# Gated mix of windowed attention and token MLP on one core: a new written-out order of tasks and PSUM banks

## Chip, cores and metric

The kernel runs on one core of a Trainium2 chip, in bf16 with float32 sums in PSUM. The metric is the device time of one execution in microseconds (us). The core's engines are TensorE (PE in the profile; its weight loads are PEld), VectorE (DVE), ScalarE (ACT), GpSimd (POOL) and SyncE (SP), which here issues all DMAs.

## The reference

Two branches read the same x of 2048 tokens by 512 channels and are mixed by a gate per token. Branch A is attention with 32 heads of 16 channels, in which a token sees itself and the 255 tokens before it. Branch B normalises each token, then multiplies along the token axis: 2048 to 1376, gelu, 1376 to 2048.

```python
x = A_x
g = sigmoid((x * gate_w).sum(-1, keepdims=True))
# A
qkv = x @ wqkv                       # 2048 x 1536, 32 heads of 16
scores = q @ k.T * 16 ** -0.5        # per head
scores = where((i - j >= 0) & (i - j < 256), scores, -1e9)
a = (softmax(scores) @ v) @ wo
# B
h = layernorm(x)                     # over the 512 channels
u = gelu(einsum("bsd,sf->bdf", h, w1) + b1)
b = transpose(einsum("bdf,fs->bds", u, w2) + b2)
out = g * a + (1 - g) * b
```

## The kernel before

**Tiles.** Tokens are worked in 16 tiles of 128 and four blocks of 512. x is loaded as it is (`xo`, four tiles to a load) and transposed (`XT`: block 0 by TensorE, tasks `xta` and `xtc`, blocks 1 to 3 by DMA transposes, tasks `xt1` to `xt3`). `wqk0` to `wqk3` and `wv` load the projection weights, `w1_gi` the first MLP weights (group g of columns, block i of rows), `w2_g` the second ones into the same memory once the `u` chains of that group are done, `wo` the output weights.

**Tasks.** The program is a list of named tasks, each on one engine:

- `q k v`: projection chains, four matmuls into one PSUM bank, in pieces of two (`q1_2.0` and `q1_2.2` are quarter 1 of the channels for block 2; block 0's pieces are single matmuls, `.0` to `.4`). `qc`, `kc` and `vc` copy a chain's bank out; `qc` (DVE) spreads q over heads in `QZ`.
- `s{j}.v0` to `v3`, `s{j}.C`: scores of attention step j, whose 128 queries begin at 128 j + 64, with full key tiles (visits) and with the corners of the window; each fills two pairs of PSUM banks. `e` (ACT) takes the exponential of a pair, `m` (DVE or POOL) masks it, `pv{j}.0` to `.3` multiply with v. `n1`, `n2`, `nz`, `n3`, `n4` (DVE) normalise and write the result back into `xo`.
- `vs` and `vz` are small DMAs that place copies of v for the corners. They wait for value copies, on SP's queue.
- `bs`, `ba` (DVE) and `pow` (POOL) make the layernorm's mean and deviation, `h` (DVE) the normalised tile. `gate0` (TensorE) and `gl` (DVE) make the gate's sums, `gatee` its exponential; `biast` and `biasc` turn the biases into columns, and `gate0` waits for `biasc`.
- `u0` to `u10`: the first MLP product, 16 matmuls each in pieces of two, needing all 16 `h` and a whole group of w1. `ub` adds the bias. `gelu` is one task on ACT for all of them.
- `y0` to `y14`, `y15l`, `y15r`: the second MLP product (11 matmuls) and the attention's output product (4 matmuls, which wait for `n4`) in one bank; `f` applies gate and bias, `o` stores.

**Order.** It isn't left to a scheduler. `PLAN` (line 189) lists for each engine every task in order; digits behind a colon are the PSUM banks or buffers that it takes. `arrange` (line 85) walks these lists with planned durations and interleaves the engines' lists into one order of emission; the order within an engine is the list's. Where two engines use one PSUM bank after each other, the later one waits.

**Pieces in tiles.** A chain's piece that stands behind a score or pv task named in `THEN` is issued as matmuls of 32 weight columns, four times as many (`tiled[0]` in `chain`, lines 645 to 676), which avoids a change of array mode after pv. The matmuls of all chains carry line 670, of scores 942 (998 for the last step), of corners 1042, of pv 1087.

**Instruction blocks.** In `arrange`, `count` adds up TensorE's instructions, and a block of 256 that is planned to arrive late delays the planned start:

```python
while (block + 1) * BLOCK <= count + ins:
    block += 1
    at = start + t.cost * (block * BLOCK - count) / ins
    wait = max(0.0, come.get(block, 0.0) - at)
```

Of the kernel before, what the change touches and what calls it, by code (L numbers as in the profile page):

```python
# [9 lines left out]
ACT = mybir.ActivationFunctionType  # L10
# [68 lines left out]
SWITCH = 0.095  # L79

BLOCK, AHEAD, FETCH, BUSY = 256, 80, 3.6, 3.0
LATENCY = {"PE": 0.22, "ACT": 0.15, "DVE": 0.12, "POOL": 0.15, "SP": 2.0}


def arrange(tasks):
# [18 lines left out]
    mode, then = "d", "d"  # L104
    count, come, loads = AHEAD, {}, 0.0
    order = []
    while len(order) < len(tasks):
# [19 lines left out]
        t.cost = t.engines[e]  # L127
        ins = t.ins
        if e == "PE":
            new = then if t.flex else t.mode  # L130
            if new != mode:
                t.cost += SWITCH
            if t.flex and new == "p":
                t.tiled = True
                ins *= 4
            if t.mode != "d":
                then = "p" if t.name in THEN else "d"
            mode = new
        if e == "SP" and t.lat is not None and t.engines[e] > 1.0:
            loads = max(loads, start + t.cost + t.lat)  # L140
        if ins:
            block = count // BLOCK
            while (block + 1) * BLOCK <= count + ins:
                block += 1
                at = start + t.cost * (block * BLOCK - count) / ins
                wait = max(0.0, come.get(block, 0.0) - at)
                t.cost += wait
                come[block + 1] = at + wait + FETCH + (BUSY if at + wait < loads else 0.0)
            count += ins
# [41 lines left out]
        warm:3 xta0.0.0:7 xta0.0.1:6 warmb xta0.1.1:4 xta0.1.0:5 q1_0.0:2 k3_0.0:3 k1_0.0:6 q3_0.0:1 k0_0.0:7  # L191
        q3_0.1 q0_0.0:0 k3_0.1 q1_0.1 q1_0.2 k1_0.1 k3_0.2 k0_0.1 q0_0.1 q2_0.0:5 q1_0.3 q0_0.2 q1_0.4 q0_0.3
        k3_0.3 q3_0.2 q0_0.4 k3_0.4 q3_0.3 k2_0.0:4 q2_0.1 k0_0.2 k1_0.2 k1_0.3 k0_0.3 k1_0.4 q2_0.2 q3_0.4 q2_0.3
        k0_0.4 k2_0.1 k2_0.2 k2_0.3 k2_0.4 q2_0.4 s0.v0:62 q3_1.0:0 q3_1.2 k3_1.0:1 k3_1.2 q0_1.0:7 s0.C:42 v1.0:6
        q0_1.2 s-1.C:02 v1.2 v2.0:5 v2.2 s1.v3:02 biast:4 v0.0:7 v0.2 v3.0:5 v3.2 q1_1.0:4 s1.v0:62 v5.0:1 q1_1.2
        gate0:5 v5.2 v14.0:0 s0.v1:62 v13.0:5 k2_1.0:1 v14.2 pv-1.0:6 v10.0:4 k2_1.2 v13.2 s1.v2:26 k2_2.0:0 v10.2
        v15.0:1 v12.0:5 v12.2 v15.2 k2_2.2 pv0.0:2 pv0.1 s1.v1:64 pv0.2 v4.0:1 v4.2 k3_2.0:0 k3_2.2 s2.v1:26 v7.0:5
        v7.2 k0_2.0:4 s1.C:60 k0_2.2 v6.0:3 v6.2 s2.v3:06 k0_1.0:2 k0_1.2 k1_1.0:5 k1_1.2 pv1.0:6 pv1.1 pv1.2
        s2.v0:02 v11.0:4 v11.2 v8.0:5 v8.2 pv1.3 pv1.4 s2.v2:20 q2_1.0:5 v9.0:4 q2_1.2 s2.C:26 v9.2 k1_2.0:1 k1_2.2
        u3.0:0 u3.2 s3.v1:64 u3.4 u3.6 u3.8 s3.C:26 u3.10 u3.12 u3.14 u2.0:1 s3.v2:24 pv2.0:6 pv2.1 u7.0:0 pv2.2  # L200
        pv2.3 u7.2 u2.2 s3.v0:42 u2.4 u7.4 u7.6 s3.v3:46 u7.8 u7.10 u7.12 s4.v0:62 u2.6 u2.8 u2.10 u2.12 u2.14
        s4.v1:24 pv3.0:6 pv3.1 pv3.2 pv3.3 u7.14 u10.0:1 u10.2 s5.v2:42 u10.4 u10.6 u10.8 s4.v3:62 u10.10 q0_2.0:0
        q0_2.2 s4.v2:64 u10.12 u10.14 q3_2.0:2 u0.0:3 q3_2.2 s4.C:06 u0.2 u0.4 u0.6 s6.v0:40 u0.8 u0.10 u0.12
        u6.0:2 u0.14 s5.v0:06 pv4.0:4 pv4.1 pv4.2 pv4.3 u6.2 u6.4 q2_2.0:3 s5.v1:06 u6.6 q2_2.2 u6.8 s5.C:64 u6.10
        u6.12 u5.0:3 s6.C:60 u6.14 u5.2 u5.4 s6.v2:46 u5.6 k3_3.0:2 k3_3.2 q1_2.0:1 q1_2.2 u5.8 s5.v3:46 u5.10
        u1.0:2 u1.2 s6.v1:06 u1.4 pv5.0:4 u5.12 pv5.1 pv5.2 pv5.3 s6.v3:06 u1.6 u5.14 u1.8 s7.v0:64 u1.10 pv6.0:0
        pv6.1 pv6.2 u1.12 pv6.3 s7.v1:64 u1.14 u4.0:3 u4.2 s7.v3:06 u4.4 k1_3.0:2 k1_3.2 s7.C:04 u4.6 u4.8 q0_3.0:2
        s7.v2:60 q0_3.2 u4.10 u4.12 u4.14 s8.v3:46 u9.0:2 u9.2 u9.4 s8.C:04 u8.0:3 u8.2 u8.4 u8.6 s8.v1:46 u8.8
        u9.6 u9.8 s8.v0:04 u8.10 u9.10 u9.12 u8.12 u8.14 s8.v2:06 pv7.0:4 u9.14 pv7.1 pv7.2 pv7.3 s10.v0:02
        k0_3.0:7 k0_3.2 q1_3.0:4 q1_3.2 q3_3.0:6 k2_3.0:5 k2_3.2 q3_3.2 pv8.0:0 pv8.1 pv8.2 pv8.3 y4.0:3 q2_3.0:6  # L210
        q2_3.2 y0.0:7 y0.2 y0.4 y8.0:2 y0.6 y4.2 y0.8 s9.v1:40 y4.4 y8.2 y0.10 y8.4 y0.11 y0.13 s9.v3:40 y4.6 y4.8
        y4.10 y4.11 s9.v2:60 y4.13 y8.6 y8.8 s9.C:04 y7.0:3 y8.10 y7.2 y8.11 s9.v0:60 y7.4 y8.13 y7.6 s10.C:46 y7.8
        y2.0:2 y2.2 s10.v3:06 y2.4 y7.10 y2.6 y7.11 s11.v3:46 y2.8 y7.13 pv9.0:0 pv9.1 pv9.2 pv9.3 s10.v2:64 y2.10
        y2.11 y9.0:3 y9.2 s10.v1:04 y2.13 y9.4 y9.6 s11.C:60 y9.8 y1.0:2 y1.2 s11.v2:40 y1.4 y1.6 y9.10 y1.8
# [12 lines left out]
        e-1.C.0:b vc1 vc2 e1.v3.1:2 e1.v3.0:3 vc3 e1.v0.0:6 e1.v0.1:9 vc5 gatee0 e0.v1.0:d e0.v1.1:c vc14 kc2_1
        vc13 e1.v2.1:b e1.v2.0:7 vc12 vc15 kc2_2 e1.v1.0:5 e1.v1.1:a vc4 e2.v1.1:4 e2.v1.0:8 e1.C.1:d e1.C.0:c vc7
        vc6 e2.v3.1:1 e2.v3.0:0 kc1_1 e2.v0.1:a e2.v0.0:9 vc8 vc11 e2.v2.0:b e2.v2.1:5 e2.C.1:e vc9 e2.C.0:f
        e3.v1.0:c e3.v1.1:d e3.C.0:7 e3.C.1:6 ub3 e3.v2.0:a e3.v2.1:4 e3.v0.0:b e3.v0.1:5 e3.v3.1:f e3.v3.0:e  # L230
        e4.v0.1:1 e4.v0.0:0 e4.v1.0:b e4.v1.1:4 ub7 e5.v2.1:f e5.v2.0:e e4.v3.0:a e4.v3.1:d e4.v2.0:5 ub10
        e4.v2.1:c e4.C.0:2 e4.C.1:3 e6.v0.1:9 e6.v0.0:8 gatee1 e5.v0.1:0 e5.v0.0:1 e5.v1.1:c e5.v1.0:d e5.C.0:4
        e5.C.1:5 e6.C.0:7 e6.C.1:6 e6.v2.1:a e6.v2.0:b kc3_3 e5.v3.1:g e5.v3.0:h e6.v1.0:2 e6.v1.1:3 gatee2
        e6.v3.1:g e6.v3.0:h e7.v0.0:f e7.v0.1:e ub5 e7.v1.0:g e7.v1.1:d e7.v3.0:h e7.v3.1:c e7.C.0:9 e7.C.1:8
        e7.v2.0:a e7.v2.1:b e8.v3.0:6 e8.v3.1:7 e8.C.1:3 e8.C.0:4 e8.v1.0:2 e8.v1.1:5 e8.v0.0:1 e8.v0.1:0 gatee3
        e8.v2.0:f e8.v2.1:e e10.v0.0:g e10.v0.1:h gelu e9.v1.1:b e9.v1.0:8 e9.v3.1:9 e9.v3.0:2 e9.v2.1:4 e9.v2.0:3
        e9.C.0:5 e9.C.1:i e9.v0.0:a e9.v0.1:j e10.C.1:6 e10.C.0:f e10.v3.1:0 e10.v3.0:c e11.v3.0:1 e11.v3.1:d
        e10.v2.1:7 e10.v2.0:e e10.v1.0:5 e10.v1.1:4 e11.C.1:3 e11.C.0:j e11.v2.1:b e11.v2.0:a e11.v1.0:i e11.v1.1:2
# [1136 lines left out]
```

## Time and profile before

| quantity | value |
|---|---|
| median of three runs | 200.57 us (199.84 to 200.81) |
| profiled execution | 199.82 us |
| its span, first to last instruction | 198.1 us |
| instructions | 9100 |
| TensorE busy, granted clock | 193.0 us (97%), 1.0 |
| ACT busy | 169.0 us (85%) |
| DVE busy | 156.5 us (79%) |
| POOL busy | 80.0 us (40%) |
| moved by DMA | 22.02 MB, mean 111 GB/s |

The profile is of one execution. Busy time is the union of an engine's instructions; matmuls overlap, so the distance from one start to the next tells more of TensorE than its busy share. A timeline line gives the start, the time covered, the engine, the line of the kernel and the operation with its shapes and count. DMA issues on SP are marked SPq; their time is that of the issue, and the landing is listed apart.

### The profile page before, as it was taken

To read this page: it belongs to the slowest core of one execution; us is meant where nothing else is said; L and a number is where in the kernel's file an instruction comes from. 1 tells how busy PE (TensorE), PEld (TensorE's weight loads), DVE (VectorE), ACT (ScalarE), POOL (GpSimd) and SP (SyncE) were. 2 spreads that over 40 slices of the span, in tenths; PEclk is the share of its full clock that TensorE was granted. 3 is DMA by queue.
4 is the path that set the end of the run, shared out by engine and by line. 5 is a ranking of instruction groups with operands and counts; after the bars stand their busy time and mean duration, and the time that the engine had idled before them with its cause. 6 is when DMAs were issued, how large, how long until landed. Compare 5 with 4: busy or idle time off the path is not lost. (4 is left out here: it accounts for less than half of the span.)

```text
span 198.1 us, 9100 instructions
## 1 busy us (share of the span) xinstructions
PE 193.0 (97%) x4058; PEld 93.3 (47%) x4058; DVE 156.5 (79%) x318; ACT 169.0 (85%) x198; POOL 80.0 (40%) x118
## 2 busy tenths in 40 slices
PE   7999999999999999999999999999999999999993
PEld 3643444353635445446543554344445354554572
DVE  1799888879998988986589799636867868869683
ACT  2369999999988996998999899899899989898632
POOL 6394897525344440214223200045069335452310
PEclk9999999999999999999999999999999999999999
DMA  5999798970060000001399770000211220200002
GB/s 156 294 284 232 131 319 278 346 187 0 8 174 18 18 0 3 3 5 32 98 364 367 280 210 3 26 26 30 68 37 58 60 68 22 62 30 30 30 3 83
DMA packets 23189, 22.02 MB, mean 111 GB/s; under 512 B 7566, under 2 KB 21262, under 8 KB 23150
## 3 DMA queue, kind: packets, MB, share of 16 engines
q1 hardware_dynamic: 23150, 21.44, 36.9%
q8 instruction: 32, 0.52, 1.1%
q14 instruction: 7, 0.06, 0.1%
HBM read 15.61 MB, written 2.10 MB: 89 GB/s over the span
## 5 line engine op out<-in xcount | busy, mean ns | idle before, releaser
L894 ACT ACTIVATE et<-ps 128x1024 bf16<-128x1024 f32 (+1 forms) x94 | 89.3, 1015 | 6.1 <-PE ps L942 2.4
L536 POOL TENSOR_SCALAR_AFFINE_SELECT et<-et 128x512 bf16<-128x512 bf16 (+2 forms) x63 | 46.7, 751 | 56.0 <-ACT et L894 40.9
L894 ACT ACTIVATE XT<-ps 128x1024 bf16<-128x1024 f32 (+1 forms) x60 | 58.1, 1011 | 7.3 <-PE ps L942 4.3
L670 PEld LDWEIGHTS <-wb 128*32 128x32 bf16 (+4 forms) x645 | 32.0, 97 | 34.5 <-issue 6.5
L670 PE MATMUL pb<-ug,wb 128*32 128x512 bf16 (+4 forms) x385 | 45.5, 366 | 0.0
L670 PE MATMUL pb<-h,wb 128*128 128x512 bf16 (+2 forms) x260 | 44.5, 381 | 0.0
L536 POOL TENSOR_SCALAR_AFFINE_SELECT XT<-XT 128x512 bf16<-128x512 bf16 (+1 forms) x28 | 20.0, 720 | 46.3 <-ACT XT L894 27.4
L670 PE MATMUL pb<-XT,wqkv 128*128 128x512 bf16 (+2 forms) x190 | 32.4, 372 | 0.4 <-DMA wqkv<-in_A_wqkv_dram 0.3
L1178 DVE STREAM_TRANSPOSE et<-ps 128x1024 f32<-128x1024 f32 (+1 forms) x17 | 20.1, 1183 | 11.9 <-PE ps L1087 11.1
L1087 PEld LDWEIGHTS <-VA 128*32 128x32 bf16 (+1 forms) x1056 | 20.1, 97 | 6.6 <-issue 1.5
L942 PE MATMUL ps<-QZ,KT 32*128 32x256 bf16 (+1 forms) x496 | 23.1, 265 | 0.0
L754 DVE TENSOR_TENSOR QZ<-pb,par 128x1024 bf16<-128x1024 f32 x16 | 19.5, 1221 | 3.2 <-PE pb L670 3.2
L670 PEld LDWEIGHTS <-wqkv 128*128 128x128 bf16 (+1 forms) x190 | 12.7, 98 | 14.6 <-DMA wqkv<-in_A_wqkv_dram 0.5
L670 PE MATMUL pb<-wo,xo 128*32 128x512 bf16 (+2 forms) x152 | 18.1, 375 | 0.0
L1087 PE MATMUL ps<-et,VA 128*32 128x128 bf16 (+2 forms) x624 | 17.9, 218 | 0.0
L942 PEld LDWEIGHTS <-KT 32*128 32x128 bf16 x496 | 7.4, 92 | 20.6 <-ACT et L894 10.7
L670 PE MATMUL pb<-wqkv,XT 128*128 128x512 bf16 (+1 forms) x70 | 16.5, 381 | 0.0
L974 DVE TENSOR_TENSOR et<-et,mask 128x512 bf16<-128x512 bf16 x26 | 13.3, 510 | 2.5 <-ACT et L894 2.4
L441 DVE TENSOR_SCALAR ot<-pb,c,c 128x512 bf16<-128x512 f32 (+1 forms) x11 | 8.6, 785 | 7.4 <-PE pb L670 7.3
L1087 PE MATMUL ps<-XT,VA 128*32 128x128 bf16 (+2 forms) x432 | 13.9, 215 | 0.0
L1087 PEld LDWEIGHTS <-VZ 128*32 128x32 bf16 x832 | 13.2, 98 | 0.7
L770 DVE BATCH_NORM_STATS2 stats<-xo 128x6 f32<-128x512 bf16 x16 | 10.7, 682 | 3.1 <-DMA xo<-in_A_x_dram 3.1
(76 smaller groups left out, 199.4 us busy)
## 6 DMA issues: line engine op xcount, KB each, us to landing
wb<-in_B_w_dram SPq DMA_DIRECT2D x8, 512.0 KB, 8.2
wb<-in_B_w_dram SPq DMA_DIRECT2D x2, 2048.0 KB, 9.2
VZ<-VA SPq DMA_DIRECT2D x26, 70.0 KB, 3.0
xo<-in_A_x_dram SPq DMA_DIRECT2D x3, 512.0 KB, 5.5
out_dram<-ot SPq DMA_DIRECT2D x12, 128.0 KB, 2.4
wb<-in_B_w_dram SPq DMA_DIRECT2D x4, 352.0 KB, 5.8
wqkv<-in_A_wqkv_dram SPq DMA_DIRECT2D x4, 256.0 KB, 5.0
wb<-in_B_w_dram SPq DMA_DIRECT2D x1, 1024.0 KB, 5.3
```

Of the source, the lines that this page charges most:

```text
L441: return nc.vector.tensor_scalar(out=out_, in0=in_, scalar1=scale, scalar2=bias, op0=ALU.mult, op1=ALU.add)
L536: return nc.gpsimd.affine_select(out=out_, in_=in_, pattern=[[0, n] for n in pattern] + [[step, HB]], compare_op=op, fill=0.0, base=base_, ...
L670: made.append(nc.tensor.matmul(buf(b)[c:z_, c0:c0 + w_], lhsT=lhsT[:, c:z_], rhs=rhs, start=(j == 0), stop=(j == n - 1), skip_group_check= ...
L754: lambda k=k, b=b: nc.vector.tensor_tensor(out=QZ[:, k, :, (i % NQ) * SB:(i % NQ + 1) * SB], in0=buf(b)[:, None, :].to_broadcast([P, 2, SB ...
L770: f"bs{t_}", {"DVE": 0.67}, lambda b=b, t_=t_: nc.vector.bn_stats(buf(b)[:], xo[:, t_, :]),
L894: lambda e=e, b=b, shape=shape: nc.scalar.activation(out=shape(buf(e)), in_=shape(buf(b)), func=ACT.Exp, scale=SCALE),
L942: made.append(nc.tensor.matmul(to[:, :, done:done + m], lhsT=keys(j if x == "A" else j - 1, k)[rows], rhs=q[rows], start=True, stop=True, ...
L974: made.append(nc.vector.tensor_tensor(out=v, in0=v, in1=m.to_broadcast(list(v.shape)), op=ALU.mult))
L1087: return lambda: nc.tensor.matmul(to(), lhsT=v() if callable(v) else v, rhs=buf(e)[rows, col:col + n], start=first, stop=last, tile_positi ...
L1178: lambda: nc.vector.transpose(out=view(buf(tr).bitcast(FP32)), in_=view(buf(o))), [last], takes=[tr], uses=[o],
```

## The change

All five lists of `PLAN`, the bank and buffer digits in them, and `THEN` are replaced. So are the constants with which `arrange` plans: the cost of a change of array mode becomes a table by pair, task costs are corrected by `cost_of`, and the arrival of an instruction block is planned from the row that asks for it (77 rows ahead of the block) and needed 194 rows inside it, with a longer fetch while a large load runs. Planned durations of some loads, of `vs`/`vz`, of `gelu` and of the w2 loads change. No task is added or removed, and the code that emits instructions is the same.

```diff
-SWITCH = 0.095
-BLOCK, AHEAD, FETCH, BUSY = 256, 80, 3.6, 3.0
-LATENCY = {"PE": 0.22, "ACT": 0.15, "DVE": 0.12, "POOL": 0.15, "SP": 2.0}
+TURN = {
+    "d": dict(d=0, s=0.100, p=0.100, c=0.098, h=0.100),
+    "s": dict(d=0.116, s=0, p=0.115, c=0.105, h=0.114),
...
+}
+BLOCK, AHEAD, INSIDE, FETCH, BUSY = 256, 77, 194, 4.0, 2.4
+LATENCY = {"PE": 0.21, "ACT": 0.15, "DVE": 0.11, "POOL": 0.12, "SP": 2.3}
+def cost_of(t, e):
+    c, n = t.engines[e], t.name
+    if e == "PE":
+        return c - 0.02 if t.mode == "s" else c * 0.738 if t.mode == "c" else c
+    if e == "DVE":
+        return max(0.1, c - 0.06)
...
-            block = count // BLOCK
-            while (block + 1) * BLOCK <= count + ins:
...
+            for k in range(1, int(x1 / BLOCK) + 2):
+                at = BLOCK * k - AHEAD
+                if x0 <= at < x1:
+                    asked[k] = start + t.cost * (at - x0) / (x1 - x0)
...
     SP="""
-        x0.0 x0.2 wqk0 wqk1 wqk2 wqk3 x1.4 xt1 wv x2.8 bias xt3 x3.12 xt2 vs0 w1_02 w1_03 vs1 w1_22 vs2 gw w1_12
-        w1_23 w1_01 w1_00 w1_10 w1_11 vz2:0 w1_13 vz3:1 vz4:2 vz5:0 w1_20 w1_21 vz6:1 vz8:0 w2_0 vz7:2 w2_1 w2_2
+        x0.0 x0.2 wqk0 wqk1 x1.4 wqk2 wqk3 x2.8 wv xt1 bias xt3 x3.12 vs0 xt2 vs1 w1_21 w1_20 w1_03 w1_01 gw
+        vz2:1 vz4:0 vs2 w1_02 w1_12 w1_00 w1_22 w1_11 w1_10 vz3:2 vs13 w1_13 w1_23 vz7:1 vz5:2 vz6:0 w2_0
...
     PE="""
-        k0_0.4 k2_0.1 k2_0.2 k2_0.3 k2_0.4 q2_0.4 s0.v0:62 q3_1.0:0 q3_1.2 k3_1.0:1 k3_1.2 q0_1.0:7 s0.C:42 v1.0:6
+        q0_0.4 k3_0.2 k3_0.3 k3_0.4 q2_0.3 q2_0.4 q3_0.2 q3_0.3 q3_0.4 s0.v0:06 v2.0:2 v1.0:5 v2.2 v0.0:4
+        v1.2 s0.C:06 v5.0:3 v5.2 v0.2 k2_1.0:2 s-1.C:06 q3_1.0:5 q3_1.2 k2_1.2 s1.v3:06 v14.0:3 v4.0:4 v14.2
+        v4.2 biast:5 v3.0:2 s1.v0:06 v3.2 q1_1.0:4 q1_1.2 v12.0:7 gate0:6 v12.2 pv-1.0:0 s0.v1:24 k0_2.0:6
...
     DVE="""
+        ba6 ba5 qc2_0 qc3_0 bs4:1 bs9:0 ba4 bs8:1 vc5 ba9 ba8 bs0:0 bs11:1 qc3_1 ba11 m-1.C.1 m-1.C.0 ba0
+        bs15:1 bs14:0 vc14 biasc ba15 ba14 qc1_1 gatem0 n1-1:c bs10:1 ba10 kc0_2 h4 bs12:0 h6 n2-1 qc0_1 ez0
+        n10:2 ba12 kc1_1 h9 h11 bs13:1 nz-1:1 h8 n3-1:1 n20 vc13 m2.v1.1 h10 h3 m1.C.1 m1.C.0 m2.v1.0 ba13
+        h1 n11:8 h2 h5 h0 kc1_2 h14 h15 h12 h7 qc2_1 h13 m2.v0.1 nz0:0 vc9 vc8 n30:0 gl11 m2.C.0 gl13
...
     ACT="""
+        xtc0.0.1 xtc0.1.1 kc1_0 kc2_0 kc0_0 kc3_0 e0.v0.1:6 e0.v0.0:3 vc2 e0.C.0:2 e0.C.1:1 vc1 e-1.C.1:8
+        e-1.C.0:0 vc0 kc2_1 e1.v3.0:9 e1.v3.1:5 vc4 e1.v0.1:4 e1.v0.0:7 vc3 vc12 e0.v1.1:a e0.v1.0:0
...
-    gelu = add("gelu", {"ACT": 8.3}, emit_gelu, ub)
+    gelu = add("gelu", {"ACT": 7.0}, emit_gelu, ub)
```

At the end of the lists, `f14`, `f15l` and `f15r` stand on DVE (`f14` and `f15l` stood on ACT), and TensorE's last pieces are `y15r.8 y15l.8 y15l.10 y15l.11 y15l.13 y15r.10 y15r.11 y15r.13` in place of `y15r.6 y15r.8 y15l.11 y15l.13 y15r.10 y15r.11 y15r.13`. Before `gelu`, ACT has `e8.v2.0 e8.v2.1 ub9 e10.v0.1 e10.v0.0`.

## Prediction

> **What bounds the kernel now.** I read the page's busy times first, then TensorE's waits, then TensorE's timeline and the DMA queue's.
>
> The page, part 1, and the list of what TensorE waited for:
>
> ```profile
> PE 193.0 (97%) x4058; PEld 93.3 (47%) x4058; DVE 156.5 (79%) x318; ACT 169.0 (85%) x198; POOL 80.0 (40%) x118
> ```
> ```profile
> PE pb L591 <- DVE ug L518: 1.4, 1, 1.4
> PE pb L670 <- DMA wqkv<-in_A_wqkv_dram: 0.3, 1, 0.3
> PE pb L670 <- ACT XT L894: 0.2, 1, 0.2
> ```
>
> Busy TensorE alone proves little, but the waits add up to 1.9 us of 198.1. Whether the busy part is full is read from start times:
>
> ```profile
> 33.23 1.03 PE L670 MATMUL pb<-XT,wqkv 128*128 128x512 bf16 x4
> 34.19 0.40 PE L942 MATMUL ps<-QZ,KT 32*128 32x256 bf16 x8
> 34.52 1.04 PE L670 MATMUL pb<-wqkv,XT 128*128 128x512 bf16 x4
> ```
>
> Four 512-column matmuls take 0.96 us to the next start: 4 x 0.216 plus 0.10 for the turn to the score matmuls (L942), which take 0.33 with their turn back. I did this for every task of the PE list, start to next start. The groups hardly scatter: a two-matmul piece 0.430, before s/c/pv tasks 0.526; a tiled piece (eight matmuls of 32 columns) 0.437, before s/c 0.54; a visit's scores 0.33 whatever follows; two-sided corners 0.36; pv with 16 matmuls 0.227, with 48 0.457, and 0.10 more if scores or an untiled piece follow.
>
> From the first L670 matmul (6.57) to the last piece (194.62) are 188.05 us. Counts times durations give 187.38. So stalls are 0.67 us: 0.16 at 6.57 until the clock is full (granted from 6.92), 0.25 at 112.98 (s10.v0, then k0_3, whose bank ScalarE had just emptied), 0.13 at 142.85, the rest under 0.1 each. **TensorE is full; the kernel is a sum of its pieces**, plus 6.57 us of start, set by the landing of wqk0, and 3.5 us of tail.
>
> **What the Trainium skill says.** "TensorE: Matmul & The Clock Gate", Back-to-back issue gap, gives N/2.4 + 2.5 ns; the trace agrees (215 to 216 ns for 512 columns). "TensorEngine Tiling (Array Packing)", Key Properties, says that changing the tiling mode drains TensorE; the 0.10 us turns agree. "Runtime: NRT & Kernel Launch", Instruction fetch mechanics, has 16 KiB blocks of 256 instructions, mostly hidden; the trace has 32 such packets:
>
> ```profile
> q8 instruction: 32, 0.52, 1.1%
> ```
>
> "DMA: Bandwidth & Descriptors", Queues, rings and completion order, says that each of SP's rings consumes descriptors in order; here a transpose issued at 4.23 first moved a packet at 8.14, behind the loads ahead of it.
>
> **The change, part by part.**
>
> *Model constants* (TURN, cost_of, FETCH, LATENCY): the chip sees none of them. Per-engine orders, banks and THEN are written out; the constants only move planned starts, which decide the interleaving in emission and the shared-port waits of POOL. Cost 0; bound +-0.2 for a port wait more or less.
>
> *TensorE's order.* The work is the same, so only turns count. Paid turns (0.10 us) before: 57 from untiled pieces into s/c/pv, 16 from tiled pieces into s/c, 13 from pv into scores or untiled pieces: 86. After: 59 + 11 + 11 = 81, so -0.50. The bias transpose no longer follows scores at 0.23 in place of 0.33: +0.10. The sum over all groups is **-0.42** (tiled pieces, 74 to 69, are in it). The stalls after 112 belong to old neighbours; if none returns, **-0.51**. The 0.16 of clock stays.
>
> *Instruction blocks.* From the row that stands 77 ahead of a block's start to the packet's end took 2.0 us in the median, up to 4.9 under w1/w2 loads. The room until 194 rows into the block was never under 3.2 us before, and none stalled. With the same durations the new order leaves 3.9 or more; only two blocks lie under loads: the third (5.3 us of room, 4.4 taken before) and the 16th (3.9, 2.9 taken). 0 to 0.6 us; I take 0.1.
>
> *ScalarE, VectorE, GpSimd.* 23 masks move from POOL to DVE: 19 visits x 0.45, 3 corners at 0.42 to 0.77, one whole at 0.77; value copies on DVE 2 to 5 (x 0.69), XT copies 1 to 2 (0.41), ub 7 to 5 (x 0.75): DVE +12 us, ACT -1 (two ub at 0.70 in, three value copies at 0.62 and one XT copy at 0.60 out), POOL -18. Hidden under TensorE while DVE keeps up: it was 87 to 93% busy from 20 to 60 us, so this cover is thin there.
>
> *SP's order and the load phase.* Issue and landing now:
>
> ```profile
> 4.23 5.73 SPq L463 DMA_TRANSPOSE XT<-in_A_x_dram  x1
> 10.01 0.57 SPq L475 DMA_DIRECT2D wqkv<-in_A_wqkv_dram  x1
> 10.63 0.51 SPq L454 DMA_DIRECT2D xo<-in_A_x_dram  x1
> ...
> 12.69 3.23 SPq L463 DMA_TRANSPOSE XT<-in_A_x_dram  x1
> 15.96 0.58 SPq L454 DMA_DIRECT2D xo<-in_A_x_dram  x1
> 16.59 4.29 SPq L463 DMA_TRANSPOSE XT<-in_A_x_dram  x1
> 21.39 0.54 SPq L718 DMA_DIRECT2D VS<-VA  x1
> ```
>
> The transposes landed 7.8, 5.3 and 6.4 us after issue. The first four issues (x0.0, x0.2, wqk0, wqk1) stay, so the start at 6.57 does. Laying the new PE list out with the durations above gives when each load is needed:
> - x1.4 goes ahead of wqk2 and wqk3 (+1.6 us for them); they are now first used at 9.8 and 10.7, formerly 8.6 and 9.0. Free.
> - x2.8 and wv go ahead of xt1. By the page's rates (156, 294, 284 GB/s per 4.95 us) the 3.0 MB ahead of xt1 have moved by 12.6: wv is there by 13.6 (needed 14.15), XT1 by about 16.0 (needed 16.67, v5). Free by half a us.
> - xt3 now follows xt1 with only the bias loads between; x2.8's packets, which filled that gap, are gone. Issue of xt1 ends some 1.5 us before its last packet (9.96 against 11.56 in the trace), so near 13.9; four bias issues 1.4; xt3 at 15.3 lands at 20.6. Needed at 20.48 (v14): 0 to 0.3.
> - x3.12 follows at 18.6, landing 4.5 to 5.1 later, near 23.4 (21.1 now). DVE reaches bs15 at about 21, so it idles 2.4 us, and behind bs15 stand bs14, vc14 and biasc (0.61 + 0.61 + 0.61 + 0.27): biasc ends near 25.5, and gate0 on TensorE, due at 24.92, waits for it: 0 to 1.0.
> - vs0 is now ahead of xt2. It waits for vc0, behind e-1.C on ACT: s-1.C ends 18.8, its two 512-column exps and vc0 end at 20.7; vs0's two issues take 1.22 (21.39 to 22.61 in the trace); xt2 at 22.0, lands 5.3 later at 27.3. It is needed at 26.42 by k0_2: 0.2 to 1.0, with a landing of 4.5 to 5.3.
>
> The last two overlap, since a wait at gate0 shifts k0_2 too: I take **+0.8** for both, range 0.2 to 1.3, and +0.1 for XT3.
>
> *gelu.* s10.v0 ends 112.87; with ub9 ahead, its exps (0.94 each) end near 115.1, the table load (1.28) and two pieces (1.48, 1.9) by 119.7, and y0.2 wants it at 119.67: +0.1.
>
> *Tail.* The last pieces are the same, and f15l moves from ACT (0.56) to DVE (0.55), done as y15r.13 ends: 0 to +0.1.
>
> Sum: -0.42 - 0.51 + 0.1 + 0.8 + 0.1 + 0.1 = **+0.17 us** on the profiled execution's 199.82 (span 198.1 and 1.7 around it). The median shown, 200.57, lies 0.75 above that one; I carry the difference over: 200.7.
>
> **The rivals.**
> 1. *The floor is reached*: all loads arrive in time, -0.93, 199.6. For it: most slacks are half a us and landings are uncertain by as much. Against: XT2 and x3.12 both come out late.
> 2. *A DVE debt makes it slower.* From bs15 to h13, the last h, DVE has 22.8 us of spaced work (5 bs, 16 h, 3 q copies at 1.15 and the rest). From 21.0 it ends at 43.8; u3.0, which needs all h, is due at 46.67. With bs15 at 23.4 it ends at 46.2 without one idle moment, and qc2_1 inside it waits for TensorE anyway. It decides once x3.12 lands after about 24: each further us goes to TensorE. 1 to 2 us on top of +0.17: 201.8 to 202.8. For it: DVE's 90%; against: the queue drains faster if nothing is behind it.
> 3. *Nothing happens*: constants invisible, turns -0.4, stalls as before: 200.2. Against: all queues did change.
>
> **How the numbers follow.** Forecast 0.50 (-0.4 to +0.9), floor 0.16, nothing 0.08, debt and other late waits 0.26. TensorE's floor is -0.93 us, -0.46%, so faster by over 0.5% (1.0 us, about what a measurement of this kernel can tell from no change) needs a start earlier too: 0.06. The debt case is the slower one: 0.26. Range 199.6 (floor) to 202.3 (middle of the debt).
>
> **What would show it.** Right: TensorE waits of 0.3 to 1 us for DVE (gate0) or for XT at 24 to 28; no stall over 0.2 in 50 to 110; DVE near 168 busy; score and pv groups unchanged in mean. Wrong: the first L670 matmul away from 6.6; stalls in the last third from masks or PSUM release; u3.0 waiting for h; an instruction block as the end of an idle gap.

## The result, and the profile after

Run in turn on one chip, the changed kernel has a median of **200.70 us** (199.86 to 202.78, 20 runs) and the kernel before one of 200.15 us (199.50 to 200.81, 20 runs). The ratio is 1.004, its 95% interval 1.0022 to 1.0058: slower by 0.2 to 0.6%. The medians alone give 1.0027; the ratio is higher because after's times have a long upper tail (four of its 20 runs are above 201.5 us, none of before's). An execution more than 1.5% above the fastest of its kernel is left out of the ratios; that was one, in e8 (203.35 us). The profiled execution took 200.29 us, with a span of 198.6; before it was 199.82 and 198.1. So the two profiles differ by 0.47 us, the medians by 0.55, and the first can be used to explain the second.

The page of after, the busy times and the queue of TensorE's instruction blocks, of which 31 packets came:

```profile
PE 193.4 (97%) x4026; PEld 93.2 (47%) x4026; DVE 160.0 (81%) x343; ACT 167.9 (85%) x196; POOL 58.8 (30%) x92
q8 instruction: 31, 0.51, 1.1%
```

POOL gave up 21 us of work, DVE took 3.5, and TensorE is as full as it was. Its list of waits has two entries; the columns are the total in us, the number of waits, and the longest.

```profile
PE pb L624 <- DVE ug L551: 1.2, 1, 1.2
PE ps L1120 <- issue: 0.6, 1, 0.6
```

The first lies ahead of the first load's landing, as it did before (1.4), and is not on the path. The second is new. "issue" means that TensorE waited for nothing that the profile records: neither a semaphore nor a transfer of data.

As for the prediction, I went through TensorE's tasks by their starts, and called a stall what a task takes beyond its usual distance to the next start (0.05 us and more). The row of the pieces is what is left after the stalls.

| us | before | after | difference |
|---|---|---|---|
| first projection matmul | 6.57 | 6.06 | -0.51 |
| pieces, their turns included | 187.36 | 187.05 | -0.31 |
| stalls until the clock is full | 0.16 | 0.37 | +0.21 |
| other stalls | 0.53 | 1.62 | +1.09 |
| last piece starts | 194.62 | 195.10 | +0.48 |

The tail, 3.5 us, and what lies around the span, 1.7, are unchanged. **The turns are saved and the old stalls are gone, and new stalls cost more than both.** Of the 1.62, 0.77 is one gap inside pv8, and 0.85 is eight short waits, each at a place where the new order lets TensorE arrive just before ScalarE or VectorE is done: 0.12 at s0.v0 (13.2), 0.15 at k1_1.0 (31.9), 0.16 at pv7.0 (109.5), 0.10 at pv9.0 (135.8), 0.14 at s12.C (161.7) and less elsewhere. The one at k1_1.0 stands so in the timeline of weight loads of after:

```profile
32.50 0.11 PEld L703 LDWEIGHTS <-wqkv 128*128 128x128 bf16 x2 [0.48 <-ACT et L927]
```

Not all of the 0.48 is lost, since loads run ahead of the matmuls. The piece in front of biast takes 0.10 more than one in front of another piece, too; I count it as a turn, because it is 0.09 to 0.10 in every profile of this order, whatever piece stands in front.

The gap in pv8, in the timeline of TensorE's weight loads in after:

```profile
115.25 0.16 PEld L1120 LDWEIGHTS <-VZ 128*32 128x32 bf16 x8
115.33 0.10 PEld L1120 LDWEIGHTS <-VA 128*32 128x32 bf16 x3
116.17 0.09 PEld L1120 LDWEIGHTS <-VA 128*32 128x32 bf16 x1 [0.73 <-issue]
116.17 0.12 PEld L1120 LDWEIGHTS <-VZ 128*32 128x32 bf16 x6
```

A run of equal weight loads is cut after the third, and the fourth starts 0.8 us later without having waited for data. In before the same loads of pv8 run through without a gap:

```profile
117.44 0.16 PEld L1087 LDWEIGHTS <-VZ 128*32 128x32 bf16 x8
117.53 0.11 PEld L1087 LDWEIGHTS <-VA 128*32 128x32 bf16 x4
117.55 0.16 PEld L1087 LDWEIGHTS <-VZ 128*32 128x32 bf16 x8
```

Count TensorE's instructions as the trace has them, each load, each matmul and each semaphore instruction as a row, and every 256 of them as a block. The cut is then at row 194 of the 16th block, the row at which the plan too has the block needed. The count starts at the first recorded instruction, so its zero is a convention: 124 rows of the 16th block had run before the 16th packet even began, and what that packet brought is taken to begin at row 194, where TensorE stops. The trace does not record when a packet is asked for; I take the start of the row 77 ahead of the block, which is the plan's constant. By that, the packet was asked for at about 111.4, began at 113.63 and ended at 114.60. While it waited, `w2_2`, issued in two parts at 109.21 and 112.51, was on its way.

### The profile page after: what moved, and what is told of

Read it like the earlier page. It is cut to its first block, busy times and chain, and to the rows that moved or that the text cites. A ratio compares the mean times of both kernels' runs of the same rounds, so it can differ in the third digit from the quotient of the medians.

```text
span 198.6 us, 9001 instructions
## 1 busy us (share of the span) xinstructions
PE 193.4 (97%) x4026; PEld 93.2 (47%) x4026; DVE 160.0 (81%) x343; ACT 167.9 (85%) x196; POOL 58.8 (30%) x92
## 4 chain that ended last, share of the span: by engine, by line
PE 91%; DMA 3%; DVE 2%; SPq 1%; issue 1%; DVEq 0%
PE pb L703 67%; PE ps L1120 11%; PE ps L975 10%; DMA xo<-in_A_x_dram 3%; PE ps L1075 3%; DVE stats L803 1%; DVE QZ L787 1%; SPq L487 0%; SPq L503 0%; PE ps L1031 0%; DVE ot L474 0%; PE pb L835 0%; DVE par L603 0%; DVE mv L807 0%; PE pb L589 0%
## 5 line engine op out<-in xcount | busy, mean ns | idle before, releaser
L927 ACT ACTIVATE et<-ps 128x1024 bf16<-128x1024 f32 (+1 forms) x100 | 95.8, 1014 | 7.7 <-PE ps L975 4.3
L927 ACT ACTIVATE XT<-ps 128x1024 bf16<-128x1024 f32 (+1 forms) x54 | 53.6, 1024 | 4.3 <-PE ps L975 2.2
L569 POOL TENSOR_SCALAR_AFFINE_SELECT et<-et 128x512 bf16<-128x512 bf16 (+2 forms) x47 | 31.4, 679 | 83.1 <-ACT et L927 54.5
L703 PEld LDWEIGHTS <-wb 128*32 128x32 bf16 (+4 forms) x637 | 31.9, 97 | 35.5 <-issue 6.5
L703 PE MATMUL pb<-ug,wb 128*32 128x512 bf16 (+6 forms) x337 | 44.8, 370 | 0.0
L703 PE MATMUL pb<-h,wb 128*32 128x512 bf16 (+2 forms) x300 | 44.1, 381 | 0.0
L703 PE MATMUL pb<-XT,wqkv 128*128 128x512 bf16 (+2 forms) x166 | 32.1, 373 | 0.0
L569 POOL TENSOR_SCALAR_AFFINE_SELECT XT<-XT 128x512 bf16<-128x512 bf16 (+1 forms) x18 | 14.3, 800 | 42.5 <-ACT XT L927 26.3
L1211 DVE STREAM_TRANSPOSE et<-ps 128x1024 f32<-128x1024 f32 x15 | 18.7, 1249 | 9.8 <-PE ps L1120 6.8
L1120 PE MATMUL ps<-et,VA 128*32 128x128 bf16 (+2 forms) x688 | 21.8, 217 | 0.6 <-issue 0.6
L703 PEld LDWEIGHTS <-wqkv 128*128 128x128 bf16 (+1 forms) x166 | 12.4, 99 | 13.4 <-issue 0.8
L703 PE MATMUL pb<-wo,xo 128*32 128x512 bf16 (+2 forms) x158 | 17.5, 374 | 0.0
L703 PE MATMUL pb<-wqkv,XT 128*128 128x512 bf16 x64 | 16.4, 380 | 0.0
L1120 PE MATMUL ps<-et,VZ 128*32 128x64 bf16 x512 | 13.8, 193 | 0.0
L1120 PEld LDWEIGHTS <-VZ 128*32 128x32 bf16 x832 | 13.2, 98 | 0.7
```

What stands on the lines that cost most here:

```text
L569: return nc.gpsimd.affine_select(out=out_, in_=in_, pattern=[[0, n] for n in pattern] + [[step, HB]], compare_op=op, fill=0.0, base=base_, ...
L703: made.append(nc.tensor.matmul(buf(b)[c:z_, c0:c0 + w_], lhsT=lhsT[:, c:z_], rhs=rhs, start=(j == 0), stop=(j == n - 1), skip_group_check= ...
L927: lambda e=e, b=b, shape=shape: nc.scalar.activation(out=shape(buf(e)), in_=shape(buf(b)), func=ACT.Exp, scale=SCALE),
L1120: return lambda: nc.tensor.matmul(to(), lhsT=v() if callable(v) else v, rhs=buf(e)[rows, col:col + n], start=first, stop=last, tile_positi ...
L1211: lambda: nc.vector.transpose(out=view(buf(tr).bitcast(FP32)), in_=view(buf(o))), [last], takes=[tr], uses=[o],
```

## The experiments

A plan's line is shown with `-` as in the kernel after (in e4 and e12: before) and `+` as run. In the kernels with an edited list and in e11 the lines are five lower than in after (L698, L970, L1070, L1115), in e5 four; e4 and e12 have those of before. All ratios are to the kernel before, timed in turn with it. The letters in the expectations name theories within one expectation or the ones next to it.

### e1: pv8 away from the load

```diff
 PE
- q2_3.2 pv8.0:6 pv8.1 pv8.2 pv8.3 q3_3.0:1 k0_3.0:0 k0_3.2 q1_3.0:5 q1_3.2 q3_3.2 y4.0:2
+ q2_3.2 q3_3.0:1 k0_3.0:0 k0_3.2 q1_3.0:5 q1_3.2 q3_3.2 pv8.0:6 pv8.1 pv8.2 pv8.3 y4.0:2
```

> The changed kernel with one edit: pv8.0 to pv8.3 stand behind q3_3.2 in TensorE's list instead of ahead of q3_3.0, so that six two-matmul pieces lie between the two dense groups pv7 and pv8. Theory A (instruction block): the 0.77 us in pv8.1 is TensorE running out of instructions 189 rows into block 16; with 2.6 us more ahead of that row the stall goes, and the spread of the runs shrinks with it. Expected: no gap over 0.2 us in pv8, last piece 0.7 to 0.8 us earlier relative to the first projection matmul, ratio to before 1.000 (0.998 to 1.002) instead of 1.004. Theory B (the stall is a wait for a mask, a VZ copy or a PSUM bank of pv8, shown as nothing): the gap moves along with pv8.1 and stays above 0.5 us, ratio 1.003 to 1.005.

Measured: 202.17 us, ratio 1.0106 (1.0069 to 1.0142). The gap in pv8 is gone. In its place stand two waits that TensorE's timeline names:

```profile
116.36 2.94 PE L698 MATMUL pb<-XT,wqkv 128*128 128x512 bf16 x12 [0.60 <-DVE et L1206]
124.57 0.40 PE L970 MATMUL ps<-QZ,KT 32*128 32x256 bf16 x8 [1.10 <-DVE QZ L782]
```

q3_3.0 comes some 1.5 us earlier than it was planned and finds its bank not yet emptied by DVE's normalisation after pv7 (0.76 over the usual distance); and DVE, whose list has n18 for pv8 ahead of the q copies, brings `QZ` for s9.v1 too late (1.17). The packet of block 16 came as late as in after (2.2 us after it was asked for), but TensorE, with slower pieces to work on, was not yet there. So the gap needs the dense pv groups at that moment; moving four tasks past six costs more than it.

### e2: less of w2

```diff
- nc.sync.dma_start(w2[:, lo:hi, :], B_w2[lo * P:hi * P, :].rearrange("(t p) s -> p t s", p=P))
+ hi_ = hi if not g else lo + 1
+ nc.sync.dma_start(w2[:, lo:hi_, :], B_w2[lo * P:hi_ * P, :].rearrange("(t p) s -> p t s", p=P))
```

> The changed kernel with less of the second weight loads: of groups 1 and 2 of w2 only the first 128 rows are loaded (and the last 96), so part of the second MLP product uses other data; every other instruction is as in the changed kernel. Theory A1 (the block comes late because the large loads are in the DMA queues when it is asked for): packet of block 16 some 1 us earlier, stall in pv8.1 0 to 0.2 us, ratio to before 0.999 to 1.001. Theory A2 (the rows alone are too dense, two pv groups within 4 us): the stall stays at 0.5 to 0.8 us, ratio 1.003 to 1.005.

Measured: 200.57 us, ratio 1.0026 (1.0009 to 1.0043). Of w2's groups 1 and 2 this kernel loads the first 128 rows and the last 96 and leaves out the rest, so it can only serve as a probe. The order is that of after to the last task, only bytes are missing, and the gap in pv8 is gone; the packet of block 16 now began 0.9 us after it was asked for, in place of 2.2. So the gap belongs to the load, as theory A1 has it. But the time hardly falls (A1 expected 1.001 at most), since a wait that the gap had covered comes to light:

```profile
124.56 0.40 PE L975 MATMUL ps<-QZ,KT 32*128 32x256 bf16 x8 [0.61 <-ACT et L927]
```

s9.v3 needs a pair of banks that ScalarE empties with its first exp after gelu (0.68 over the usual distance). In after ScalarE's chain reads:

```profile
115.32 1.28 ACT L1286 ACT_TABLE_LOAD   x1
116.61 4.66 ACT L1286 ACTIVATE ug<-ug 128x1536 bf16<-128x1536 bf16 x3
121.17 0.61 ACT L1288 ACTIVATE ug<-ug 96x512 bf16<-96x512 bf16 x1
121.81 1.28 ACT L927 ACT_TABLE_LOAD   x1
123.10 1.02 ACT L927 ACTIVATE et<-ps 128x1024 bf16<-128x1024 f32 x1
```

From the first table load to the first exp are 7.78 us, and the new plan counts 7.0 for `gelu` (8.3 before the change). TensorE arrives at s9.v3 0.7 us too early, which fits; no run changes the constant alone. In after, the gap in pv8 had held it up by as much just before.

### e3: SP's old head in the new kernel

```diff
 SP
- x0.0 x0.2 wqk0 wqk1 x1.4 wqk2 wqk3 x2.8 wv xt1 bias xt3 x3.12 vs0 xt2 vs1
+ x0.0 x0.2 wqk0 wqk1 wqk2 wqk3 x1.4 xt1 wv x2.8 bias xt3 x3.12 xt2 vs0 vs1
```

> The changed kernel with SP's first 15 entries in the order of before (wqk2 and wqk3 ahead of x1.4, xt1 ahead of wv and x2.8, xt2 ahead of vs0). Tells apart whether the earlier start (first projection matmul at 6.06 us, 6.57 before) is due to that order. Theory C (it is the order: wqk0 shares the queues with less behind it): first projection matmul back at 6.5 to 6.6. Theory D (it is the luck of one execution): it may lie anywhere from 6.0 to 6.6, as in all other runs. Either way wv lands near 14.5 and v2, due at 13.9, waits 0.5 to 1.0 us: ratio to before 1.006 to 1.011.

Measured: 201.88 us, ratio 1.0082 (1.0049 to 1.0115), the first projection matmul at 6.17. That is within the scatter of the other profiles, so the order of SP does not set the start. The ratio lies in the expected range, but the wait of v2 for wv, on which that range was built, did not come. x1.4 is now late for DVE, whose new list wants it early (timeline of DVE, then of TensorE):

```profile
9.52 0.69 DVE L798 BATCH_NORM_STATS2 stats<-xo 128x6 f32<-128x512 bf16 x1 [1.71 <-DMA xo<-in_A_x_dram]
...
12.00 1.21 DVE L782 TENSOR_TENSOR QZ<-pb,par 128x1024 bf16<-128x1024 f32 x1
```
```profile
14.39 0.40 PE L970 MATMUL ps<-QZ,KT 32*128 32x256 bf16 x8 [1.00 <-DVE QZ L782]
```

A `bs` at the head of DVE's queue waits 1.71 us for x1.4, the q copy behind it is late, and s0.v0 waits 1.07. The gap in pv8 is there again, at 1.00.

### e4: x1.4 early in the kernel before

```diff
 SP
- x0.0 x0.2 wqk0 wqk1 wqk2 wqk3 x1.4 xt1 wv
+ x0.0 x0.2 wqk0 wqk1 x1.4 wqk2 wqk3 xt1 wv
```

> The kernel before with one edit: x1.4 is issued between wqk1 and wqk2, as in the changed kernel. Theory C (that order lets wqk0 land earlier): first projection matmul at 6.0 to 6.1 instead of 6.57, but wqk2 and wqk3, first used at 8.6 and 9.0, land 0.5 to 1.5 us late: ratio to before 1.000 to 1.004. Theory D (luck): start between 6.0 and 6.6 with no pattern, and the same waits for wqk2: ratio 1.001 to 1.006.

Measured: 201.62 us, ratio 1.0079 (1.0057 to 1.0101), slower than either theory had it, with the first projection matmul at 5.87. TensorE waits for wqk2, 1.05 over the usual distance:

```profile
9.44 1.26 PE L670 MATMUL pb<-XT,wqkv 128*128 128x512 bf16 x4 [0.89 <-DMA wqkv<-in_A_wqkv_dram]
```

With e3, this shows the two lists as one piece: x1.4 ahead of wqk2 fits the new TensorE and DVE lists and not the old, and the reverse.

### e5: room behind gelu

```diff
 as e2, and PE
- y0.6 s9.v3:46 y0.8 y0.10 y0.11 y0.13 s9.v2:06 y4.10 y4.11 y4.13
+ y0.6 y0.8 y0.10 s9.v3:46 y0.11 y0.13 y4.10 y4.11 s9.v2:06 y4.13
```

> The kernel of e2 (less of w2 loaded, so part of the second MLP product uses other data) with s9.v3 two pieces later (behind y0.10) and s9.v2 two pieces later (behind y4.11) in TensorE's list. Theory E (with the block's stall gone, ScalarE's chain e10.v0, table load, gelu, table load, e9.v1 sets the time: s9.v3 waits 0.68 us in e2 for a PSUM pair that e9.v1 empties): the wait at s9.v3 falls to 0.1 us or less, the last piece comes 0.5 to 0.6 us earlier relative to the first projection matmul, ratio to before 0.999 to 1.001 (e2: 1.0026). Theory F (s9.v3 waited for something of the load of w2): the wait moves with s9.v3, ratio as e2.

Measured: 201.48 us, ratio 1.0062 (1.0039 to 1.0086). The wait at s9.v3 is gone, and yet the median lies 0.9 above e2's. s9.C waits 0.40 for ScalarE 3 us later (the corners' exps are behind those of s9.v3 and s9.v2), and at 187.4 TensorE stands still for 0.7 us with "issue" named, where no w2 load runs. That one is an instruction block again, the 29th; its packet came soon (0.7 us after it was asked for) and took 1.37 us where most take about 1. I had not thought of a block there. The exchange as such need not cost time: e10 has it too and is no slower than e9.

### e6: w2's last group later

```diff
 SP
- vz8:2 w2_2 wo vz9:1 vz10:2
+ vz8:2 vz9:1 w2_2 wo vz10:2
```

> The changed kernel with w2_2 behind vz9 (and ahead of wo) on SP's list, nothing left out: w2_2's issue moves from 109.2 to about 113.5, after block 16 has been asked for. Theory A1 (contention with the large load makes the block late): packet of block 16 near 112.5, no stall in pv8.1; instead s9.v3 waits 0.5 to 0.7 us for ScalarE's chain behind gelu, so ratio to before 1.002 to 1.004, hardly better than the changed kernel. Rival: w2_2 itself comes too late, y4.0 waits 0.5 us or more, ratio 1.004 to 1.008.

Measured: 200.62 us, ratio 1.0028 (1.0014 to 1.0042). `w2_2`'s two parts are issued at 114.83 and 115.47 in place of 109.21 and 112.51. The gap in pv8 is gone, with all bytes loaded, and s9.v3 waits 0.68: the same pair as in e2, and all that A1 expected. In this execution TensorE also waited 0.53 for projection weights at 7.3 and 0.22 for wqk2 at 9.6.

### e7: slack for the late loads

```diff
 SP
- x3.12 vs0 xt2 vs1
+ x3.12 xt2 vs0 vs1
 DVE
- ba0 bs15:1 bs14:0 vc14 biasc ba15
+ ba0 vc14 biasc bs15:1 bs14:0 ba15
```

> The changed kernel with more slack in its load phase: xt2 ahead of vs0 on SP's list, vc14 and biasc ahead of bs15 and bs14 on VectorE's. Theory G (the wider spread of the changed kernel's runs, 199.9 to 202.8, is late landings of x3.12 and XT2 that stall gate0 and k0_2 in some executions): median 0.2 to 0.5 us lower than 200.7 and spread under 1.5 us. Theory H (it comes from elsewhere, or the loads are in time): median and spread unchanged, ratio 1.003 to 1.005.

Measured: 200.78 us, ratio 1.0033 (1.0018 to 1.0048). This takes away both causes of the prediction's +0.8 (bs15's wait in front of biasc, vs0 in front of xt2), and nothing is gained, for nothing was lost there. The spread stays wide too (200.05 to 202.30), so late loads of this phase do not explain it.

### e8: six neighbours exchanged

```diff
 PE
- v4.2 biast:5 v3.0:2
+ v4.2 v3.0:2 biast:5
- v6.2 k1_1.0:6 v13.0:2 k1_1.2
+ v6.2 v13.0:2 k1_1.0:6 k1_1.2
- u8.12 pv7.0:0 u9.12 u8.14
+ u8.12 u9.12 pv7.0:0 u8.14
- y8.6 pv9.0:4 pv9.1 y7.6
+ y8.6 y7.6 pv9.0:4 pv9.1
- y7.13 y1.0:4 y1.2 y5.0:5
+ y7.13 y5.0:5 y1.0:4 y1.2
- y10.13 s12.C:60 y11.0:4
+ y10.13 y11.0:4 s12.C:60
```

> The changed kernel with six exchanges of neighbours in TensorE's list, each moving a task that waited in every execution so far behind a piece that doesn't wait: k1_1.0 behind v13.0, biast behind v3.0, pv7.0 behind u9.12, y7.6 ahead of pv9.0, y5.0 ahead of y1.0, s12.C behind y11.0. Theory I (these tasks were planned to the tenth of a us of ScalarE's and VectorE's releases, and the waits of 0.15, 0.10, 0.16, 0.10, 0.07 and 0.14 us are paid by TensorE): waits there under 0.03, last piece 0.6 to 0.7 us earlier, ratio to before 1.000 to 1.002. Theory J (ScalarE or VectorE is the bound there, so the wait only moves to the next task that needs them): total of waits unchanged, ratio 1.003 to 1.005.

Measured: 200.62 us, ratio 1.0032 (1.0014 to 1.0049). The waits at k1_1, pv7.0, pv9.0 and s12.C (0.55 in after) are gone, the turn into biast stays, with another piece in front of it. s10.v0, behind pv7, now waits 0.17, s13.C 0.28 where s12.C had 0.14, and the gap in pv8 has 0.94. What was gained before 115 is spent in waiting for the block there: its packet ended at 114.96, not sooner than in after (114.60), though TensorE was ahead.

### e9 and e10: the edits together

e9 has e6, e7 and e8 in one; e10 has e5's exchange of s9.v3 and s9.v2 as well.

> The kernel after with three edits that were each tried alone before: w2's last group behind vz9 (as in e6), the six neighbour swaps (as in e8), and xt2 ahead of vs0 with vc14 and biasc ahead of bs15 and bs14 (as in e7). The question: do small waits add up, or does each one removed only uncover the next? Theory K (they add): against after's accounting the 0.77 behind pv8.1 and the swapped waits (0.10 at biast, 0.15 at k1_1, 0.16 at pv7.0, 0.10 at pv9, 0.14 at s12.C) go, s9.v3 waits 0.68 for ScalarE; stalls from the clock's end on near 0.9 in place of 1.7, median 199.9 to 200.2. Theory J (slack is conserved: a release on ScalarE or VectorE is late by the plan's error wherever the reader stands): stalls from there on stay at 1.4 or more, median 200.5 to 200.8, with s9.v3 at 0.8 or more because what was gained ahead of the gelu chain comes back there.

> As e9, and the two scores behind gelu set back as in e5 (s9.v3 behind y0.10, s9.v2 behind y4.11). Nothing of the computation is left out. K: the 0.68 at s9.v3 goes too, stalls after the clock near 0.5, 199.6 to 199.9, the only version that would be faster than the kernel before by more than 0.2%. J: what s9.v3 no longer waits for turns up within 12 us at s9.C or y2.0 (0.4 in e5), and near 187 at y13.8 (0.7 in e5), because ScalarE works through the same chain of exps at 0.90 us each; 200.4 to 201.0, no better than e9.

Measured: e9 200.49 us, ratio 1.0040 (1.0021 to 1.0058); e10 200.51, ratio 1.0024 (1.0010 to 1.0038). In e9 the waits came as theory K had them at pv8 (none) and s9.v3 (0.67), but the stalls after the clock are about 2.0, as J had it: 0.28 for wqk2 at 9.2, 0.27 at s0.v0, 0.28 at s13.C in place of s12.C, 0.17 at s10.v0. The median is at the lower edge of J's range; s9.v3 at 0.8 or more did not come. In e10, whose time is in J's range too, s9.v3's wait went and 0.41 came at s9.C; a block, this time the third, cost 0.76 (weight loads of e10):

```profile
39.72 0.10 PEld L698 LDWEIGHTS <-XT 128*128 128x128 bf16 x1
40.69 0.33 PEld L698 LDWEIGHTS <-XT 128*128 128x128 bf16 x3 [0.88 <-issue]
```

The 0.7 at y13.8, which my text for e10 put down to ScalarE, did not come back: it had been the block named under e5.

### e11: after once more

No edit.

> The kernel after unchanged, one more profile of it, to see which of its stalls come back. Theory S (systematic): the wait behind pv8.1 is there again at 0.6 to 1.0, and gate0 and k0_2 wait less than 0.1; those two answers hold for the kernel and not for one execution. Theory R (a matter of one execution): the wait behind pv8.1 is under 0.3 here, or gate0 and k0_2 together wait 0.5 or more, as the prediction had it. The first projection matmul between 5.7 and 6.8 under both.

Measured in the one execution: 201.22 us, span 199.5. The gap is there, but one block earlier, inside pv7, and then the gelu wait isn't covered any more; both are seen (weight loads, then matmuls, of e11):

```profile
112.52 0.09 PEld L1115 LDWEIGHTS <-VA 128*32 128x32 bf16 x1 [0.56 <-issue]
```
```profile
125.18 0.40 PE L970 MATMUL ps<-QZ,KT 32*128 32x256 bf16 x8 [0.60 <-ACT et L922]
```

That is 0.60 and 0.67 (e2's wait at s9.v3) where the first profile had 0.77 alone; 0.25 for wqk2 and 0.31 at s0.v0 are added. gate0 and k0_2 wait for nothing. The expectation's first theory was right on gate0 and k0_2, and wrong in that the late block can be the 15th or the 16th.

### e12: the same cure for the kernel before

```diff
 PE
- s10.v0:02 k0_3.0:7 k0_3.2 q1_3.0:4 q1_3.2 q3_3.0:6 k2_3.0:5 k2_3.2
+ s10.v0:02 k2_3.0:5 k2_3.2 k0_3.0:7 k0_3.2 q1_3.0:4 q1_3.2 q3_3.0:6
- y9.6 s11.C:60 y9.8 y1.0:2 y1.2 s11.v2:40 y1.4
+ y9.6 y9.8 s11.C:60 y1.0:2 y1.2 y1.4 s11.v2:40
```

> The kernel before, with three neighbour exchanges in its TensorE list: k2_3.0 and k2_3.2 (bank 5, free since e8.v0) stand ahead of k0_3.0 (bank 7, which ScalarE empties as s10.v0 ends), y9.8 ahead of s11.C, y1.4 ahead of s11.v2. Everything else is as before. They answer its three waits after 100 us: 0.25 + 0.08 at k0_3 and q1_3, 0.13 at s11.C, 0.07 at s11.v2. Theory K (waits add up and can be taken away one by one): all of them go, nothing comes in their place, stalls after 20 us near 0.1, span 197.6 to 197.8 where the start is 6.57, median 199.6 to 199.8, ratio 0.9975 to 0.9985: a version ahead of both kernels. Theory J (each wait removed comes back at the next reader of the same engine's release): 0.3 or more of new waits after 110, ratio 0.9995 to 1.001.

Measured: 201.21 us, ratio 1.0045 (1.0026 to 1.0065). A miss, from a mistake of mine: pv7 takes the pair of banks 4 and 5, so bank 5 is free only after DVE's transpose behind pv7, 1.2 us later, and k2_3 waits for that. TensorE's waits in e12:

```profile
PE pb L670 <- DVE et L1178: 1.1, 1, 1.1
```

The waits at s11.C and s11.v2 are gone, but s11.v1 (0.22) and y5.2 (0.35) wait behind them. And the old order meets a late block too, the 28th, inside s14.C:

```profile
181.91 0.14 PEld L1042 LDWEIGHTS <-KT 32*64 32x64 bf16 x10 [0.52 <-issue]
```

### The blocks, over all runs

Eight profiles have one gap of this kind. By the count described above, TensorE stops at row 193 or 194 of a block in all eight, and goes on 1.3 to 1.6 us after the end of that block's packet:

| kernel, block | asked to packet's start | packet | packet's end to going on | stall |
|---|---|---|---|---|
| after, 16 | 2.2 | 0.97 | 1.57 | 0.77 |
| e3, 16 | 2.4 | 1.01 | 1.54 | 1.00 |
| e7, 16 | 2.1 | 1.01 | 1.57 | 0.71 |
| e8, 16 | 2.5 | 1.09 | 1.46 | 0.94 |
| e11, 15 | 4.6 | 1.95 | 1.40 | 0.60 |
| e10, 3 | 4.0 | 0.92 | 1.31 | 0.76 |
| e12, 28 | 1.2 | 1.24 | 1.42 | 0.59 |
| e5, 29 | 0.7 | 1.37 | 1.32 | 0.71 |

"Asked" is taken at 77 rows ahead of the block. In no block of any profile does row 194 come sooner than 1.2 us after its packet's end, stalled or not; so the time from the packet's end counts with the fetch. In the first six rows the packet was late. In e12 and e5 it came soon; there the rows are so dense that TensorE was through the 271 of them 3.8 and 3.4 us after asking, the stall included, and a fetch without a late start was not fast enough either. e4, with before's list of TensorE, has 0.19 at the place of e12's 28th block. With the w2 loads where the change put them and pv8 in its place (after, e3, e7, e8, e11), block 15 or 16 is late in five of five profiles; with less or later w2, or pv8 moved (e1, e2, e5, e6, e9, e10), TensorE waits for neither in any of six.

## Why the prediction was right, and where it wasn't

The forecast of 200.7 us and the case it came from (TensorE full, a small net change of either sign, inside 0.5%) held. The sum behind it was +0.17 us, though, and the measured one is +0.47 on the profile and +0.55 on the medians. **That 200.7 was met so closely is luck, twice over.** The median shown for before, to which I carried the difference, was 200.57, and 200.15 when timed in turn. And the terms of the sum erred in opposite directions: the +0.9 of the load phase did not come, while the block cost 0.77 in place of 0.1, and eight short waits that I set at nothing cost 0.85. By the signs that I had named, the mechanism was wrong in this: the waits at 24 to 28 and DVE near 168 did not come, but an instruction block at the end of an idle gap, a first L670 matmul (L703 in after) away from 6.6 and small waits for PSUM releases in the last third did. It was right in that no stall over 0.2 came between 50 and 110. Point by point:

- **TensorE's turns, -0.42.** Measured -0.31, what is left of the pieces after the stalls. The count of pairs of neighbours held but for one turn: biast no longer follows scores, and I booked the +0.10 of the scores in front, but not the 0.10 that the piece now in front of biast pays.
- **Old stalls, -0.51.** The four places no longer stall. The step said "if none returns", and that condition failed: the new order has eight short waits of its own, 0.85 us together, and those I set at nothing. They are systematic: k1_1.0, pv7.0, pv9.0 and s12.C wait 0.10 to 0.16 in every profile that keeps their neighbours. I had compared times of need with landings for the loads and not for the releases of PSUM banks by ScalarE and VectorE.
- **Instruction blocks, +0.1 of 0 to 0.6.** This was the worst-sized term: 0.77. I had named the right block and found its room (3.9 us) and what a block had taken in that region before (2.9), but counted the fetch only to the packet's end. The runs show 1.3 to 1.6 us more until TensorE goes on. 2.9 + 1.45 is 4.35 against 3.9, so the same numbers would have given a stall of about 0.45. (The least room in before, too, is 3.05 us by the trace, not 3.2.) "Runtime: NRT & Kernel Launch", Instruction fetch mechanics, in the Trainium skill calls the cost of crossing a block mostly hidden; before shows it hidden, after does not.
- **Start unchanged at 6.57.** In after 6.06. Over the profiles of after's family it lies between 5.96 (e7) and 6.92 (e8), and e4 and e12 show 5.87 and 6.33 with before's lists, so this is scatter of executions; e3 rules out SP's order as its cause. Part of a gain is lost again, because the clock is full only at 6.9 in either profile and pieces ahead of that are longer (0.37 against 0.16).
- **Load phase, +0.8 at gate0 and k0_2, +0.1 for XT3.** This step failed. It rested on landings, and those on the durations of issue in before (3.23 and 4.29 us for xt3 and xt2). SP's timeline in after:

```profile
5.50 7.19 SPq L496 DMA_TRANSPOSE XT<-in_A_x_dram  x1
...
14.31 2.00 SPq L496 DMA_TRANSPOSE XT<-in_A_x_dram  x1
16.36 0.58 SPq L487 DMA_DIRECT2D xo<-in_A_x_dram  x1
...
21.53 1.94 SPq L496 DMA_TRANSPOSE XT<-in_A_x_dram  x1
```

  Both transposes occupy SP for 2 us, so x3.12 goes out at 16.36 in place of 18.6, and its packets end at 20.6 in place of 23.4; XT2's end at 25.0, not at 27.3. A transpose's issue is long when loads are queued ahead of it: xt1, with 3 MB ahead, took 7.19. The runs that move loads on SP's list show the same: with the old head, in e3, the three take 5.00, 3.17 and 3.51, near the 5.73, 3.23 and 4.29 of before, and in e7, e9 and e10, where xt2 follows x3.12 at once, xt2 takes 3.9 to 4.6. Such a duration belongs to the queue's state, not to the operation. Of the kernels with this order of loads only e1 shows a wait at gate0 (0.13) or just ahead of k0_2 (0.17). What the load phase does cost is elsewhere, and not in each execution: up to 0.3 at q1_0.3 for wqk2, which I had called free, and 0.1 to 0.3 at s0.v0 for `QZ`.
- **gelu, +0.1.** I looked at y0.2, which reads gelu's result, and it is in time. What is late is the exp behind gelu, and s9.v3 for it: 0.68, hidden in after behind the block, in plain sight in e2, e6, e9 and e11.
- **DVE +12, POOL -18.** Measured +3.5 (160.0 busy, not 168) and -21. The masks did move, but each got shorter (groups of before, then of after; the last two numbers ahead of the second bar are busy us and mean ns):

```profile
L974 DVE TENSOR_TENSOR et<-et,mask 128x512 bf16<-128x512 bf16 x26 | 13.3, 510 | 2.5 <-ACT et L894 2.4
L974 DVE TENSOR_TENSOR XT<-XT,mask 128x512 bf16<-128x512 bf16 x18 | 8.1, 447 | 0.7 <-ACT XT L894 0.5
```
```profile
L1007 DVE TENSOR_TENSOR et<-et,mask 128x512 bf16<-128x512 bf16 x37 | 15.2, 418 | 3.9 <-ACT et L927 3.9
L1007 DVE TENSOR_TENSOR XT<-XT,mask 128x512 bf16<-128x512 bf16 x26 | 10.8, 428 | 2.0 <-ACT XT L927 1.9
```

  Nineteen more masks cost 26.0 - 21.4 = 4.6 us. In the trace of before, DVE masks of this line that overlap a POOL mask take 0.67 us in the mean (13 of them), the others 0.41 (31); after has 8 overlapping ones of 63, and its others take 0.41 too. "SBUF — State Buffer", SBUF: two separate sides, describes a port that these two engines lock for a whole instruction, which fits. No run moves the masks alone, so the gain is read from the traces only.
- **The rivals.** The DVE debt did not come: x3.12 was not late, u3.0 did not wait for h (e3 has 0.26 at s3.v1, next to it), and DVE had more room than I gave it. The floor of -0.93 was not reached by any version. "Nothing happens" had the wrong sign (200.2, -0.4, for a measured +0.55): it was right on the turns, but the stalls are not those of before.

**What stays open.** After's times reach up to 202.78, those of before 201.4 at most in all its runs. e11 shows one mechanism, a block that is late where it covers nothing, worth some 0.6 us more; it doesn't explain 2 us. e6 was narrow (200.27 to 200.98, 12 runs), but e9 and e10, with the same order of the w2 loads, go up to 202.5 and 202.6. No version in this study is ahead of the kernel before.

## What to carry to other kernels

Where one engine is full, a reordering is priced by what its neighbours release: list, for each task, the time at which its bank, its operand and its instructions are there, and compare all three with the time at which the engine will ask. A stall that is removed pays only if no other of its size stands behind it; here a late instruction block and a late exp each cost 0.7 us, and after paid for one of them in its first profile and for both in e11. A plan that is tight to a tenth of a microsecond is worth no more than its worst constant (7.0 for 7.78 at `gelu`).

## What the runs showed of the hardware

- Dense runs of short matmuls outran the supply of instructions. By the count above TensorE stopped at row 193 or 194 of a block of 256, and went on 1.3 to 1.6 us after the end of that block's packet. In six of the eight cases the packet began 2.1 to 4.6 us after the assumed request (77 rows ahead), in two 0.7 and 1.2; in e2, without most of w2, block 16's began after 0.9. Eight stalls of 0.6 to 1.0 us.
- The issue of a DMA transpose held SP's queue from 1.8 to 7.4 us for transposes of one size, by what was queued ahead: XT2's took 1.94 in after and 3.94 in e7, with x3.12 issued just ahead of it.
- From the table load ahead of gelu to the first exp behind it 7.78 us passed, 2 x 1.28 of it in the two table loads.
